# Longer DRAM rows for weight sums and second gate, a margin behind each load's landing in the planner, and 512-column warm-up products, in an attention and two-layer MoE kernel

## The chip, the cores and the metric

One core of one Trainium2 chip. The metric is the device time of one execution in microseconds; the time of a kernel is the median of its runs.

## What is computed

Random-feature attention, whose output is the input of two dense layers in a row. Sizes: 4 batches, 8 heads, 576 tokens, head width 64, 128 features; 2304 tokens of width 512, and an inner width of 2048. All data are fp32. Cut to what matters:

```python
def phi(x):
    proj = np.einsum('bhsd,md->bhsm', x, omega)
    sq = np.sum(x * x, axis=-1, keepdims=True) / 2.0
    h = proj - sq
    h = h - np.max(h, axis=-1, keepdims=True)
    return np.exp(h) / np.sqrt(m)
q_p, k_p = phi(q * scale), phi(k * scale)
kv = np.einsum('bhsm,bhsd->bhmd', k_p, v)
z = np.sum(k_p, axis=2)
num = np.einsum('bhsm,bhmd->bhsd', q_p, kv)
den = np.einsum('bhsm,bhm->bhs', q_p, z)[..., None] + 1e-06
x = (num / den)                      # tokens x 512
...
g = softplus(x @ w_in1);  x = g @ w_out1
g = silu(x @ w_in2);      out = g @ w_out2
```

## The kernel before

**Precision.** PE multiplies in a rounded fp32 form, so each factor is split into a high part (a cast on ACT) and a low part (a subtraction on DVE, `diff`, L285), and each product is three PE products, high·high, high·low and low·high.

**Stages.** Attention comes first. For a batch's keys, pp_k (L579) projects on the features, DVE reduces maxima (L596) and sums of squares (L554), ACT takes the exponential, and pkv (L291) gathers phi·v. For its queries, pp_q, a flip by PE (pq, L745), num (pn, L291), a normalization on DVE (xn, L771) and a transposition back (px, L779) give x in the layout that layer 1 needs. `first_layer` (L849 to 851, tile h) is a plain product of x with w_in1; ACT copies h out of PSUM (L855) and a store puts it to DRAM as `gate[0]`. Attention of batch b+1 is interleaved with layer 1 of batch b.

The other three products use Winograd's scheme: 7 products of 2×2 blocks instead of 8, with combined factors. `second_product(0)` (PE L977) multiplies the softplus of gate 0 with w_out1 and leaves its result in `y_dram`; `first_product` (L1225) multiplies that with w_in2, copies s1, s5, s2 out of PSUM on ACT (L1235), takes the silu and stores `gate[1]`; `second_product(1)` (L983) multiplies gate 1 with w_out2 and writes the output. Each runs the products in the order 1, 5, 6, 2, 7, 3, 4, into the PSUM tiles X, Z and Y. Second products run in NQ = 2 halves of the inner width, each over SC = 3 strips of tokens; a half loads 7 tiles w from `ws` and for each strip 4 tiles b from `gate` (768 KB each, KQ = 4 rows of a pair per partition).

**Sums of weights.** For the three Winograd products `sums_of` makes the 7 combined factors once: it unpacks the raw 64-bit words of two weight chunks to fp32 (DVE and ACT), forms sums (DVE), casts the high part (ACT L456, or L454 with a sign), subtracts the low part (DVE L285), and stores the parts to `ws[m]` in DRAM, m = (0,1), (1,0), (1,1). There are 24 such pairs. In the first APART = 12 of them a store holds 4 or 3 of the 7 factors, in the others 1 or 2. Names: st_11_0_4 is factor 4 of pair 0 of m = (1,1).

**The order of the work.** All instructions of SP, ACT, DVE and PE are added to a list with a cost, a due time and the buffers that they take; class `Order` plays the list against its costs, picks at each step the item with the least due time among those that can start, and the instructions are emitted in the order that comes out. Each engine then runs its own instructions strictly in that order. SP issues nearly all DMAs. In the plan, one wire carries them one after the other, `nbytes / RATE` each, and a DMA ends `ARRIVE` behind its wire time:

```python
if it["nbytes"]:
    wire = max(wire, free[e]) + it["nbytes"] / RATE
    it["end"] = wire + ARRIVE
```

Buffers come in rings by tag (`BUFS`): 2 of "rw", 4 of "ph", 5 of "b2", 4 PSUM banks each of "bank" and "y", and so on; an instruction that opens a tile waits for the last user of the one that held its place. Constants at the top steer the order: `STAY` (PE's inclination to stay with one kind of product), `SLACK`, `FROM`, `EARLY` (how many input tiles take the ring "wa"), `TRAIL`, `EVERY`, `WINDOW_OF`, `FETCH` (when inputs and weights may be fetched), `BACKLOG`, `SOON`, `EARLIER` (loads), `AHEAD`, `WAIT` (projections), `SHARE`, `BEGIN` (due times of layer 1), `PREP` (due times of the sums of weights).

**Warm-up.** Before the first projection, WARM = 2 products of zeros (wz, pw, L325) run on PE while the first loads are under way.

## Time and profile before

| | |
|---|---|
| median of 3 runs | 868.63 us (866.46 to 871.35) |
| profiled execution, its own time | 866.67 us |
| its span | 864.9 us, granted clock 1.0 |
| PE busy | 851.5 us, 98% |
| DVE, ACT busy | 681.6 us (79%), 542.5 us (63%) |
| DMA | 254.54 MB, mean 294 GB/s |

How to read it: one execution, times in us from the start of the span. PE is the matmul engine and PEld its weight loads, which overlap it; DVE, ACT and POOL are the vector, scalar and general engines; SP issues DMAs. In names, a<-b is output from input, xN a count of instructions, L a line of the kernel before. In the changed kernel, the lines from 100 to 465 are numbered 3 higher, and those behind them 4 higher.

### The profile page before, as it was taken

What the parts mean: (1) busy time and instruction counts of PE and PEld (TensorE: products, weight loads), DVE (VectorE), ACT (ScalarE), POOL (GpSimd) and SP (SyncE); (2) the same over time, 40 slices, a digit from 0 to 9 for tenths busy, and PEclk for the clock granted to TensorE, in tenths of its full rate; (3) what the DMA queues carried; (4) which work ended last, traced back from release to release, by engine and by line L of the source; (5) the groups of instructions that cost most, each with busy time, mean ns of one, the idle gap of its engine ahead of it and who ended that gap; (6) DMA issues with size and microseconds to landing.
All of it is one profiled execution on the core that took longest, in us unless ns stands there. A gap on an engine that the chain in (4) does not pass through costs nothing.

```text
span 864.9 us, 17428 instructions
## 1 busy us (share of the span) xinstructions
PE 851.5 (98%) x6492; PEld 801.8 (93%) x6492; DVE 681.6 (79%) x1264; ACT 542.5 (63%) x1088; POOL 1.2 (0%) x8
## 2 busy tenths in 40 slices
PE   8899999999999999999999999999999999999998
PEld 7688888888888899999999998999999999999998
DVE  4999989969997377999799943786754899768973
ACT  6977778768765566876575444766855646543430
POOL 0000000000000000000000000000000000000000
PEclk9999999999999999999999999999999999999999
DMA  9576899899989999979995899987699997799532
GB/s 319 203 240 181 259 314 333 305 348 331 311 297 362 344 345 397 366 258 308 358 324 195 279 354 390 328 291 258 224 317 345 383 352 247 252 348 348 167 117 74
DMA packets 150293, 254.54 MB, mean 294 GB/s; under 512 B 10816, under 2 KB 82624, under 8 KB 150208
## 3 DMA queue, kind: packets, MB, share of 16 engines
q1 hardware_dynamic: 150048, 253.36, 85.0%
q8 instruction: 51, 0.84, 0.4%
q14 instruction: 34, 0.28, 0.1%
q10 hardware_dynamic: 160, 0.07, 0.0%
HBM read 152.72 MB, written 100.66 MB: 293 GB/s over the span
## 4 chain that ended last, share of the span: by engine, by line
PE 89%; DMA 5%; DVE 4%; ACT 1%; issue 1%; SPq 0%; ACTq 0%; DVEq 0%
PE X L977 12%; PE X L983 12%; PE X L1225 8%; PE h L849 8%; PE h L851 8%; PE h L850 8%; PE Z L983 6%; PE Z L977 6%; PE Z L1225 4%; PE Y L983 3%; PE Y L977 3%; PE Y L1225 2%; PE pp_q L579 2%; PE pp_k L579 2%; PE pkv_k L291 2%; PE pn_q L291 2%
## 5 line engine op out<-in xcount | busy, mean ns | idle before, releaser
L849 PE MATMUL h<-x,wt 128*128 128x512 f32 (+1 forms) x328 | 123.4, 376 | 0.0
L851 PE MATMUL h<-x,wt 128*128 128x512 f32 (+1 forms) x328 | 119.6, 365 | 0.0
L850 PE MATMUL h<-x,wt 128*128 128x512 f32 (+1 forms) x328 | 119.4, 364 | 0.0
L1225 PE MATMUL X<-x_x,w 128*128 128x384 f32 x576 | 106.6, 335 | 2.7 <-ACT s L1235 2.4
L925 ACT CAST g<-b 128x768 fp32r<-128x768 f32 x96 | 78.3, 838 | 48.4 <-PE X L983 19.2
L983 PE MATMUL X<-w,g 128*128 128x256 f32 x864 | 107.0, 283 | 0.2 <-issue 0.2
L983 PEld LDWEIGHTS X<-w,g 128*128 128x128 f32 x864 | 105.1, 192 | 0.5 <-issue 0.3
L1225 PEld LDWEIGHTS X<-x_x,w 128*128 128x128 f32 x576 | 100.2, 188 | 3.7 <-ACT s L1235 3.1
L977 PE MATMUL X<-g,w 128*128 128x384 f32 x576 | 102.9, 334 | 0.0
L977 PEld LDWEIGHTS X<-g,w 128*128 128x128 f32 x576 | 100.1, 188 | 0.0
L925 ACT CAST g<-t 128x768 fp32r<-128x768 f32 x72 | 58.8, 834 | 65.3 <-DVE t L910 38.1
L285 DVE TENSOR_TENSOR g<-b,g 128x768 fp32r<-128x768 f32 x96 | 90.0, 951 | 11.1 <-ACT g L925 11.1
L285 DVE TENSOR_TENSOR g<-t,g 128x768 fp32r<-128x768 f32 x72 | 67.5, 953 | 21.0 <-ACT g L925 20.7
L849 PEld LDWEIGHTS h<-x,wt 128*128 128x128 f32 x328 | 61.9, 189 | 10.4
L851 PEld LDWEIGHTS h<-x,wt 128*128 128x128 f32 x328 | 61.9, 189 | 10.2
L285 DVE TENSOR_TENSOR st<-pair,st 128x512 fp32r<-128x512 f32 x72 | 48.9, 686 | 27.9 <-ACT st L456 27.8
L850 PEld LDWEIGHTS h<-x,wt 128*128 128x128 f32 x328 | 62.0, 189 | 8.6
L855 ACT COPY g<-h 128x512 f32<-128x512 f32 (+1 forms) x80 | 44.1, 559 | 28.7 <-PE h L851 20.2
L456 ACT CAST st<-pair 128x512 fp32r<-128x512 f32 x72 | 44.8, 629 | 19.3 <-DMA ws<-st 7.7
L983 PE MATMUL Z<-w,g 128*128 128x256 f32 x432 | 54.0, 283 | 0.2 <-DVE g L285 0.2
L1225 PE MATMUL Z<-x_x,w 128*128 128x384 f32 x288 | 53.8, 334 | 0.0
L983 PEld LDWEIGHTS Z<-w,g 128*128 128x128 f32 x432 | 52.8, 192 | 0.4 <-DVE g L285 0.4
(113 smaller groups left out, 1457.0 us busy)
## 6 DMA issues: line engine op xcount, KB each, us to landing
w<-ws SPq DMA_DIRECT2D x42, 1024.0 KB, 7.7
b<-gate SPq DMA_DIRECT2D x48, 768.0 KB, 7.5
raw<-in_w SPq DMA_DIRECT2D x64, 512.0 KB, 6.0
ws<-st SPq DMA_DIRECT2D x36, 512.0 KB, 5.1
gate<-s SPq DMA_DIRECT2D x96, 192.0 KB, 4.6
gate<-g SPq DMA_DIRECT2D x64, 256.0 KB, 5.0
ws<-st SPq DMA_DIRECT2D x12, 1024.0 KB, 7.0
ws<-st SPq DMA_DIRECT2D x12, 768.0 KB, 5.5
```

What stands on the lines that cost most here:

```text
L285: nc.vector.tensor_tensor(o, a, b, op=ALU.subtract)
L291: nc.tensor.matmul(o[r], a[:, r], b, **flags)
L456: nc.scalar.copy(st[:, :, 0], of())
L579: nc.tensor.matmul(pp[j][:, q], s["xt"][r, c : c + P], om_sb[r, :], start=True, stop=not fold)
L849: nc.tensor.matmul(ph, wt[:, 0, cs], xt[:, 0, ts], start=(opens and cc == 0), stop=False, skip_group_check=part is not None)
L850: nc.tensor.matmul(ph, wt[:, 0, cs], xt[:, 1, ts], start=False, stop=False, skip_group_check=part is not None)
L851: nc.tensor.matmul(ph, wt[:, 1, cs], xt[:, 0, ts], start=False, stop=(cc == NCC - 1), skip_group_check=part is not None)
L855: nc.scalar.copy(s["g"][:, :w], s["h"][:, :w])
L925: nc.scalar.copy(g[:, :, 0], s[src][:, 2 * r : 2 * r + 2])
L977: nc.tensor.matmul(o[:, :HW_], w[:, 2 * r + k, a, cs], g[:, k, h], start=one, stop=(k == 1 and a == 1), skip_group_check=True)
L983: nc.tensor.matmul(o[:, a * 256 : a * 256 + 256], g[:, k, h, ts], w[:, 2 * r + k, v], start=one, stop=(k == 1 and h == 1), skip_group_chec ...
L1225: nc.tensor.matmul(s[x][:, :HW_], w[:, a, cs], xop[p][:, cc, h], start=(opens and cc == 0 and a == 0 and h == 0), stop=(cc == 1 and a == 1 ...
```

## The change

Five things:

1. `gate[1]` is laid out so that a tile b (half, i, strip, j) is one block of DRAM: a load reads rows of 6144 bytes per partition instead of four rows of 1536; the stores still write rows of 1536.
2. `ws[1,0]` is `[128, 56, 512]`: a store's 1 to 4 factors are one row of up to 8 KB per partition, and the load of 4 factors reads 8 KB per partition; the rows of neighbouring partitions lie 56 × 2 KB = 112 KB apart. The other two `ws` are `[NQ, 7, 128, KQ, 512]`: a load reads one block with rows of 8 KB, stores still write rows of 2 KB.
3. The planner's cost of a DMA takes in the length of its rows, and every DMA that starts behind 54.95 us in the plan ends `MARGIN` = 1.11 us later there.
4. Most of the planner's constants have other values.
5. The warm-up products have 512 columns instead of 384.

```diff
-STAY = 6.79
+STAY = 7.6
...
-FROM = {"PE": 4.6, "ACT": 3.4, "DVE": 2.0, "SP": 0.8}
-SLACK = 0.15
-EARLY = 6
+FROM = {"PE": 5.2, "ACT": 3.6, "DVE": 2.0, "SP": 0.8}
+SLACK = 0.09
+EARLY = 3
...
-LEAD, TRAIL, EVERY, WINDOW_OF, FETCH = 0.05, 2.2, 3.13, 25.82, 24.95
+LEAD, TRAIL, EVERY, WINDOW_OF, FETCH = 0.05, 2.42, 3.06, 18.2, 16.35
...
-BACKLOG, SOON = 0.6, 13.16
-EARLIER = (26.31, 42.98)
-APART = 12
-AHEAD, WAIT = 3.04, 4.21
+BACKLOG, SOON = 0.79, 12.44
+EARLIER = (12.06, 21.87)
+APART = 13
+AHEAD, WAIT = 3.8, 4.03
 RATE = 360e3
+PER_BYTE, PER_ROW = 2.44e-6, 6.35e-4
 ARRIVE = 2.3
+MARGIN, FIRM = 1.11, 54.95
...
+        nbytes *= RATE * (PER_BYTE + PER_ROW / row)
...
-                it["end"] = wire + ARRIVE
+                it["end"] = wire + ARRIVE + (MARGIN if s > FIRM else 0.0)
...
-    gate = [dram.tile([NQ, KQ, 2, P, B * S], F32, name=f"gate{i}") for i in range(2)]
+    gate = [dram.tile([NQ, KQ, 2, P, B * S], F32, name="gate0"), dram.tile([NQ, 2, SC, 2, P, KQ, HW_], F32, name="gate1")]
...
-    ws = {m: dram.tile([NFP, 7, P, 2 * 256], F32, name=f"ws{m[0]}{m[1]}") for m in ((0, 1), (1, 0), (1, 1))}
+    ws = {m: dram.tile([P, NFP * 7, 2 * 256] if m == (1, 0) else [NQ, 7, P, KQ, 2 * 256], F32, name=f"ws{m[0]}{m[1]}") for m in ((0, 1), (1, 0), (1, 1))}
...
-    wz = get("b2", [P, 3 * P], F32, "wz")
+    wz = get("b2", [P, 2 * T], F32, "wz")
...
-                nc.sync.dma_start(ws[m][k, g : g + rows].rearrange("o p w -> p o w"), q["st"].bitcast(F32).rearrange("p o h w -> p o (h w)"))
+                to = ws[m][:, 7 * k + g : 7 * k + g + rows] if m == (1, 0) else ws[m][k // KQ, g : g + rows, :, k % KQ].rearrange("o p w -> p o w")
+                nc.sync.dma_start(to, q["st"].bitcast(F32).rearrange("p o h w -> p o (h w)"))
...
-                    nc.sync.dma_start(s["b", i, j], gate[layer][q, :, i, :, lo:hi].rearrange("k p t -> p k t"))
+                    nc.sync.dma_start(s["b", i, j], gate[1][q, i, sc, j] if layer else gate[0][q, :, i, :, lo:hi].rearrange("k p t -> p k t"))
...
-                nc.sync.dma_start(w.bitcast(F32).rearrange("p k h w -> p k (h w)"), ws[1, 0].rearrange("k o p w -> (k o) p w")[o : o + 4].rearrange("k p w -> p k w"))
+                nc.sync.dma_start(w.bitcast(F32).rearrange("p k h w -> p k (h w)"), ws[1, 0][:, o : o + 4])
...
-                        nc.sync.dma_start(gate[1][fc // (2 * KQ), fc // 2 % KQ, fc % 2][:, lo : lo + HW_], s[key])
+                        nc.sync.dma_start(gate[1][fc // (2 * KQ), fc % 2, sc, j, :, fc // 2 % KQ], s[key])
```

Since the planner's numbers change, all four engines' orders change. Three places:

On DVE, at the start (mn the maxima of a projection pp, sqs the sums of squares, kv0 the copy of pkv), before:

```order
L596 TENSOR_REDUCE mn_k0_0_0_165<-pp_k0_0_0_122 128x4
L596 TENSOR_REDUCE mn_k0_0_1_168<-pp_k0_0_1_123 128x4
L596 TENSOR_REDUCE mn_k1_0_0_185<-pp_k1_0_0_145 128x4
L596 TENSOR_REDUCE mn_k1_0_1_197<-pp_k1_0_1_146 128x4
L596 TENSOR_REDUCE mn_k0_1_0_237<-pp_k0_1_0_199 128x4
L663 COPY kv0_98<-pkv_k0_0_187 128x260
L596 TENSOR_REDUCE mn_k0_1_1_268<-pp_k0_1_1_200 128x4
L554 TENSOR_REDUCE sqs_q0_0_278<-x_q0_0_107 128x8
L554 TENSOR_REDUCE sqs_kt0_286<-x_kt0_106 128x8
L596 TENSOR_REDUCE mn_k1_1_0_296<-pp_k1_1_0_250 128x4
```

and after the change:

```order
L600 TENSOR_REDUCE mn_k0_0_0_165<-pp_k0_0_0_122 128x4
L600 TENSOR_REDUCE mn_k0_0_1_168<-pp_k0_0_1_123 128x4
L600 TENSOR_REDUCE mn_k1_0_0_202<-pp_k1_0_0_145 128x4
L600 TENSOR_REDUCE mn_k1_0_1_206<-pp_k1_0_1_146 128x4
L600 TENSOR_REDUCE mn_k0_1_0_228<-pp_k0_1_0_177 128x4
L600 TENSOR_REDUCE mn_k0_1_1_248<-pp_k0_1_1_178 128x4
L600 TENSOR_REDUCE mn_k1_1_0_264<-pp_k1_1_0_230 128x4
L667 COPY kv0_98<-pkv_k0_0_214 128x260
L600 TENSOR_REDUCE mn_k1_1_1_292<-pp_k1_1_1_231 128x4
L558 TENSOR_REDUCE sqs_q0_0_294<-x_q0_0_107 128x8
```

The reduces of pp_k0_1 and pp_k1_1 stand ahead of the copy to kv0, and the reduce sqs_kt0 no longer stands among them (it and sqs_k3_0 come later, sqs_k3_0 behind the last xn of the first batch).

On PE, in the attention of the second batch between gemms of layer 1 (pp_q2_0 and pp_q2_1 are projections of queries, pkv_k3_1 a product of keys and values), before:

```order
L579 MATMUL pp_q2_0_1_1097<-om_sb_86,x_q2_0_761 128x128
L579 MATMUL pp_q2_0_0_1096<-om_sb_86,x_q2_0_761 128x128
L579 MATMUL pp_q2_0_1_1097<-om_sb_86,x_q2_0_761 128x128
L291 MATMUL pkv_k3_1_1113<-x_k3_1_670,phi_k3_1_0_1031 64x65 x8
L291 MATMUL pkv_k3_1_1113<-x_k3_1_670,phi_k3_1_1_1038 64x65 x8
L579 MATMUL pp_q2_1_0_1134<-om_sb_86,x_q2_1_886 128x128
L579 MATMUL pp_q2_1_1_1135<-om_sb_86,x_q2_1_886 128x128
L579 MATMUL pp_q2_1_0_1134<-om_sb_86,x_q2_1_886 128x128
```

and after:

```order
L583 MATMUL pp_q2_0_1_1062<-om_sb_86,x_q2_0_814 128x128
L583 MATMUL pp_q2_0_0_1061<-om_sb_86,x_q2_0_814 128x128
L583 MATMUL pp_q2_0_1_1062<-om_sb_86,x_q2_0_814 128x128
L583 MATMUL pp_q2_1_0_1080<-om_sb_86,x_q2_1_944 128x128
L583 MATMUL pp_q2_1_1_1081<-om_sb_86,x_q2_1_944 128x128
L583 MATMUL pp_q2_1_0_1080<-om_sb_86,x_q2_1_944 128x128
L583 MATMUL pp_q2_1_1_1081<-om_sb_86,x_q2_1_944 128x128
L583 MATMUL pp_q2_1_0_1080<-om_sb_86,x_q2_1_944 128x128
```

The two projections now stand one behind the other, and pkv_k3_1 comes later, behind the gemms h_0_4 and h_0_5. Over the whole kernel the runs of pp products fall from 33 to 29, those of pkv and pn from 36 to 34, and those of the gemm rise from 41 to 43.

On ACT, at the start of the first product of layer 2 (s1, s5, s2 copies out of PSUM and their silus, st_11_0_* the casts of the first pair of weight sums for the last product), before:

```order
L1235 COPY s2_0_2_6405<-X_0_2_6341 128x384
L1235 COPY s2_0_3_6414<-X_0_3_6356 128x384
L1245 ACTIVATE s1_0_2_6364<-s1_0_2_6364 128x384
L1245 ACTIVATE s1_0_3_6377<-s1_0_3_6377 128x384
L1245 ACTIVATE s5_0_2_6389<-s5_0_2_6389 128x384
L456 CAST st_11_0_4_6453<-pair_11_0_6130 128x2x256
L1245 ACTIVATE s5_0_3_6397<-s5_0_3_6397 128x384
L456 CAST st_11_0_2_6463<-pair_11_0_6130 128x2x256
L1245 ACTIVATE s2_0_2_6405<-s2_0_2_6405 128x384
L1245 ACTIVATE s2_0_3_6414<-s2_0_3_6414 128x384
L1251 ACTIVATE s4_0_2_6487<-X_0_2_6341 128x384
L1251 ACTIVATE s4_0_3_6498<-X_0_3_6356 128x384
```

and after:

```order
L1176 CAST x3_x2_0_6108<-r110_x2_0_5686 128x384
L1176 CAST x3_x2_0_6108<-r111_x2_0_5696 128x384
L1176 CAST x4_x2_0_6122<-tb_x2_0_5861 128x384 x2
L459 CAST st_11_0_0_6191<-pair_11_0_6058 128x2x256
L457 ACTIVATE st_11_0_6_6200<-pair_11_0_6058 128x256
L1239 COPY s1_0_0_6234<-X_0_0_6214 128x384
L1239 COPY s1_0_1_6244<-X_0_1_6226 128x384
L1239 COPY s5_0_0_6253<-Z_0_0_6237 128x384
L1239 COPY s5_0_1_6261<-Z_0_1_6246 128x384
L1239 COPY s2_0_0_6269<-X_0_0_6214 128x384
L1239 COPY s2_0_1_6278<-X_0_1_6226 128x384
L459 CAST st_11_0_4_6290<-pair_11_0_6058 128x2x256
```

The four casts st_11_0_* of that pair stood among the silus of the first and second pair of units (two of them are in the rows of before); now two stand ahead of the first copies s1, and the other two among the first pair's.

## Rows read from the trace of the kernel before

**Rows 1.** Page, busy time by engine and the chain's shares.

```profile
PE 851.5 (98%) x6492; PEld 801.8 (93%) x6492; DVE 681.6 (79%) x1264; ACT 542.5 (63%) x1088; POOL 1.2 (0%) x8
...
PE 89%; DMA 5%; DVE 4%; ACT 1%; issue 1%; SPq 0%; ACTq 0%; DVEq 0%
```

**Rows 2.** Busy time by stretch: length, each engine (instructions), PEclk, DMA share, GB/s.

```profile
0.00:20.00 20.00, 17.72 (x230) 15.26 (x230) 7.92 (x14) 13.49 (x41) 1.20 (x8) 1.00 0.94 313
20.00:46.00 26.00, 21.26 (x337) 18.04 (x336) 24.97 (x84) 24.41 (x72) 0.00 (x0) 1.00 0.63 222
46.00:120.00 74.00, 74.00 (x712) 62.25 (x710) 70.28 (x171) 56.71 (x138) 0.00 (x0) 1.00 0.73 232
120.00:300.00 180.00, 180.00 (x1494) 150.02 (x1491) 147.90 (x376) 128.34 (x309) 0.00 (x0) 1.00 0.94 331
520.00:560.00 40.00, 38.08 (x220) 37.76 (x219) 20.99 (x43) 23.46 (x51) 0.00 (x0) 1.00 1.00 362
560.00:640.00 80.00, 80.00 (x463) 80.00 (x463) 57.25 (x116) 55.56 (x119) 0.00 (x0) 1.00 0.78 267
640.00:680.00 40.00, 39.26 (x228) 38.52 (x227) 22.48 (x43) 23.33 (x49) 0.00 (x0) 1.00 1.00 349
680.00:720.00 40.00, 39.76 (x330) 39.40 (x329) 38.06 (x47) 23.97 (x41) 0.00 (x0) 1.00 1.01 364
760.00:800.00 40.00, 39.83 (x333) 39.66 (x332) 31.51 (x38) 15.19 (x20) 0.00 (x0) 1.00 1.00 344
800.00:865.00 65.00, 61.59 (x514) 61.39 (x512) 44.77 (x59) 19.09 (x24) 0.00 (x0) 0.99 0.39 119
```

**Rows 3.** PE's waits: total us, times, longest.

```profile
PE px_q L779 <- DVE xn_q L771: 3.8, 3, 1.8
```

**Rows 4.** Timeline of PE at the start: start, us, what, idle before.

```profile
1.81 2.93 PE L325 MATMUL pw<-wz,ident 128*128 128x384 f32 x4 [1.81 <-POOL ident masks.py:199]
5.21 0.80 PE L579 MATMUL pp_k<-om_sb,x_k 64*128 64x128 f32 x4 [0.47 <-ACT om_sb L320]
```

**Rows 5.** Chain of waits, 10 to 11 us: start, us, what.

```profile
10.37 0.43 PE pp_k L583 x4
...
11.08 0.22 PE pp_k L583 x4
```

**Rows 6.** Busy time, 9 to 19.2 us, columns as in rows 2.

```profile
9.00:19.20 10.20, 10.20 (x184) 9.63 (x184) 7.12 (x13) 8.86 (x31) 0.00 (x0) 1.00 1.08 369
```

**Rows 7.** Chain of waits, one reduce on DVE at 43.7 us.

```profile
43.70 0.60 DVE sqs_k L554
```

**Rows 8.** Chain of waits, short and long runs of one kind on PE.

```profile
11.75 0.61 PE pkv_k L291 x16
...
14.35 1.08 PE pkv_k L291 x32
...
181.44 1.99 PE pp_k L579 x32
...
192.90 1.09 PE pp_k L579 x16
```

**Rows 9.** Chain of waits, 519 to 540 and 667 us.

```profile
519.91 8.74 DMA ws<-st
...
530.80 8.68 DMA gate<-s
...
539.56 0.49 ACT s L1235
...
667.43 7.34 DMA b<-gate
```

**Rows 10.** Timeline of ACT, the cast at 528.7 us.

```profile
528.73 0.62 ACT L456 CAST st<-pair 128x512 fp32r<-128x512 f32 x1 [2.87 <-DMA ws<-st]
```

**Rows 11.** Page, DMA issues: count, KB each, median us to landing.

```profile
w<-ws SPq DMA_DIRECT2D x42, 1024.0 KB, 7.7
b<-gate SPq DMA_DIRECT2D x48, 768.0 KB, 7.5
```

More of the change, by code (lines that the diff above doesn't have):

```diff
@@ L95, in __init__, with add @@
         self.items = []
-    def add(self, eng, cost, fn, deps=(), due=None, alloc=(), uses=(), table=None, nbytes=0, after=0.0, loose=False, behind=None, wait=0.0, tiled=False, turn=None):
+    def add(self, eng, cost, fn, deps=(), due=None, alloc=(), uses=(), table=None, nbytes=0, after=0.0, loose=False, behind=None, wait=0.0, tiled=False, turn=None, row=2048):
         occ, lag = cost if isinstance(cost, tuple) else (cost, PIPE)
         i = len(self.items)
+        nbytes *= RATE * (PER_BYTE + PER_ROW / row)
         it = dict(
@@ L380, in unpack @@
         opens = not tf["users"]
-        a = add("SP", (ISSUE, 0), load, alloc=[traw], nbytes=P * DM * 8, after=after, due=due)
+        a = add("SP", (ISSUE, 0), load, alloc=[traw], nbytes=P * DM * 8, row=4096, after=after, due=due)
         b = add("ACT", (0.575, 0.37), scale, [a], alloc=[tf] if opens else [], uses=[traw] + ([] if opens else [tf]))
@@ L474, in stage @@
             if not q["left"]:
-                kept[m, k].append(add("SP", (ISSUE, 0), store, q["ends"], uses=[ts], nbytes=P * 256 * rows * 8, due=due))
+                kept[m, k].append(add("SP", (ISSUE, 0), store, q["ends"], uses=[ts], nbytes=P * 256 * rows * 8, row=2048 * (rows if m == (1, 0) else 1), due=due))
             return b
@@ L543, in load_v @@
                 nc.sync.dma_start(s["v", i], v)
-            lv.append(add("SP", (ISSUE, 0), load_v, rv if tw is here else [] if opens else lv[:1], alloc=[tv[i]] if opens else [], uses=[] if opens else [tv[i]], nbytes=P * VW * 4, after=after))
+            lv.append(add("SP", (ISSUE, 0), load_v, rv if tw is here else [] if opens else lv[:1], alloc=[tv[i]] if opens else [], uses=[] if opens else [tv[i]], nbytes=P * VW * 4, row=1040 if shape[1] == 4 else 2080, after=after))
         def square():
@@ L898, in load @@
                     s["b", i, j] = get("xg", [P, KQ, HW_], F32, f"b{i}{j}_{name}")
-                    nc.sync.dma_start(s["b", i, j], gate[layer][q, :, i, :, lo:hi].rearrange("k p t -> p k t"))
-                got[i, j] = add("SP", (ISSUE, 0), load, deps, alloc=[tb[i, j]], nbytes=P * n * 4)
+                    nc.sync.dma_start(s["b", i, j], gate[1][q, i, sc, j] if layer else gate[0][q, :, i, :, lo:hi].rearrange("k p t -> p k t"))
+                got[i, j] = add("SP", (ISSUE, 0), load, deps, alloc=[tb[i, j]], nbytes=P * n * 4, row=HW_ * 4 * (KQ if layer else 1))
                 if layer == 0:
@@ L1009, in load @@
                     nc.sync.dma_start(s["h", c, i, j][:, : wide[c]], part_of(c, i, j))
-                return add("SP", (ISSUE, 0), load, [partly[sc, c, i, j]], alloc=[ht], nbytes=P * wide[c] * 4)
+                return add("SP", (ISSUE, 0), load, [partly[sc, c, i, j]], alloc=[ht], nbytes=P * wide[c] * 4, row=wide[c] * 4)
             def snap(p, x, c, i, j, due):
@@ L1055, in store @@
                                 nc.sync.dma_start(out[r0 : r0 + n, cs], s["h", c, i, j][p0 : p0 + n, a * 256 : a * 256 + 256])
-                            add("SP", (ISSUE, 0), store, [e], uses=[ht], due=due + 3, nbytes=n * 1024)
+                            add("SP", (ISSUE, 0), store, [e], uses=[ht], due=due + 3, nbytes=n * 1024, row=1024)
                 return e
@@ L1103, in load_w @@
                     w = wt[p] = get(tag, [P, KQ, 2, 256], F32R, f"w2_{layer}_{q}_{p}")
-                    nc.sync.dma_start(w.bitcast(F32).rearrange("p k h w -> p k (h w)"), ws[wm][q * KQ : (q + 1) * KQ, ROW[p]].rearrange("k p w -> p k w"))
-                wload[p] = add("SP", (ISSUE, 0), load_w, [i for k in range(q * KQ, (q + 1) * KQ) for i in kept[wm, k]], alloc=[tws[p]], nbytes=P * KQ * 2048, turn=t0, after=t0 + n * each - EARLIER[layer])
+                    nc.sync.dma_start(w.bitcast(F32).rearrange("p k h w -> p k (h w)"), ws[wm][q, ROW[p]])
+                wload[p] = add("SP", (ISSUE, 0), load_w, [i for k in range(q * KQ, (q + 1) * KQ) for i in kept[wm, k]], alloc=[tws[p]], nbytes=P * KQ * 2048, row=8192, turn=t0, after=t0 + n * each - EARLIER[layer])
             for sc in range(SC):
```

20 lines of the change are left out of this document (10 added, 10 removed).

## The prediction

> **What bounds the kernel now.** I read four views, in this order. The first is the page's busy table with the shares of the chain of waits [rows 1]: PE is busy 851.5 of 864.9 us, 89% of the chain is PE's work, and DVE and ACT are far from full over the whole. So the kernel is bound by PE, and only two things can shorten it: less PE work, or less of the 864.9 − 851.5 = 13.4 us in which PE stands still. The second view, busy time by stretch, says where these lie [rows 2]: length minus PE's busy time gives 2.28 us up to 20, 4.74 from 20 to 46, nothing from 46 to 300 (two stretches full to the last digit; from 300 to 520 no stretch is shown, since it reads the same), 1.92 from 520 to 560, 0.74, 0.24 and 0.17 in the stretches at 640, 680 and 760, and 3.41 behind 800. The third, PE's waits [rows 3] and the busy time from 20 to 46 [rows 2], says what bounds the start: there DVE is busy 24.97 of 26 us, and PE's largest wait is on DVE's xn_q (3.8 us). The fourth, the chain with ACT's timeline, explains the late stall, below.
>
> Durations come from the profiled execution, whose own time is 866.67 us; the median shown is 868.63, 1.96 above it. About 0.5% (4.3 us) is what a measurement of this kernel can tell from no change.
>
> **The change part by part.** PE executes the same products before and after; what changes is their order, the warm-up, and where data lie in DRAM.
>
> (a) *DVE's start.* From 20 to 46 us DVE sets PE's pace, so a DVE instruction that is moved from ahead of the first products of layer 1 to behind them shortens this part by its duration. The order shows one: the reduce of squares sqs_k3_0 now stands behind the last xn that the first gemm needs. One takes 0.60 us [rows 7]. −0.6.
>
> (b) *PE's start.* The projections pp_k0_1 stand ahead of pkv_k0_0 now, so that DVE's reduces on them no longer wait for a product that only the copy to kv needs: a short run of pkv is 0.61 us [rows 8]. The gain reaches the end only if DVE then works earlier, and DVE's idle time from 9 to 19.2 us, 10.20 − 7.12 = 3.08 us [rows 6], is all that (b) and (c) together can take. Between 0 and −0.6 I take −0.6, since DVE waits in just this stretch.
>
> (c) *Warm-up.* Four matmul records of pw take 2.93 us at 384 columns, PE then stands 0.47 us for om_sb, and the first projections start at 5.21 [rows 4]. 512 columns cost a third more, 0.98 us, of which 0.47 fill the gap: +0.5. Against this stands PE's speed: a block of four projection matmuls takes 0.43 us up to 10.8 us and 0.22 from 11.08 [rows 5], a factor of 1.95, though the granted clock stands at 1.00 for the whole stretch [rows 2]. I read the first as the level of 1.2 GHz and the second as 2.4. The slow blocks fill 5.21 to 10.80 = 5.59 us; if the rise came with the longer warm-up at once, half of that, 2.8 us, would be saved. The ends are +0.5 (no earlier rise) and 0.5 − 2.8 = −2.3; I take −0.5, a rise some 2 us sooner, near the cautious end, because no row shows what brings the rise on.
>
> So the start gives −0.6 − 0.6 − 0.5 = −1.7.
>
> (d) *Fewer changes of kind on PE.* A run of 16 pp matmuls takes 1.09 us and one of 32 takes 1.99, so 16 more cost 0.90 and a run has 0.19 fixed; for pkv it is 0.61 and 1.08, 0.14 fixed [rows 8]. By the order, runs of pp fall from 33 to 29 and runs of pkv and pn from 36 to 34; the gemm runs between them rise from 41 to 43, which I count with these pairs and not again. They lie where PE is full from 46 to 300 [rows 2], so each counts whole: −4 × 0.19 − 2 × 0.14 = −1.0. Beside this, moved gemms could make PE wait for DVE, which is busy 70.28 of 74 us from 46 to 120 [rows 2]; I cost this at nothing, as 3.7 us of idle time cover it, and at up to +1.5 in the range if they do not.
>
> (e) *The late waits.* At 528.73 ACT's cast into st_11_0_4 has waited 2.87 us for a store ws<-st to leave its buffer [rows 10]; that store was issued at 519.91 and took 8.74 us to land. ACT then takes up what is queued behind the cast, the copies s of the first product of layer 2, whose buffers in turn wait for the store gate<-s (530.80, 8.68 us); the copy that PE needs ends near 540 [rows 9]. That is PE's 1.92 us. From 520 to 560 the DMA engines are busy all the time at 362 GB/s [rows 2], so stores land late because loads stand ahead of them, not because ACT is full (23.46 of 40). The change moves the four casts of this pair ahead of the copies and their stores some 20 us earlier, and the planner counts 1.11 us more for each landing. I take the 1.92 as gone. What is late next are the small stalls, 0.74 + 0.24 + 0.17 = 1.15 us, which hang on the same kind of landing: 667.43, a b<-gate took 7.34 us [rows 9]. The margin is made for them, but each order trades one for another; I take a quarter, −0.3. Ends: nothing gained, and −3.1. Together −2.2.
>
> (f) *Longer rows.* The 42 loads of 1 MB and the 48 of 768 KB land in a median of 7.7 and 7.5 us [rows 11], in rows of 2048 and 1536 bytes. Nearly all lies under PE's work, so a shorter transfer shows only through the waits in (e) and is not counted again: 0. If loads got slower, the cover is the free share of the stretches between full ones: 560 to 640 has a DMA share of 0.78 [rows 2], so 17.6 us of wire. The output stores behind the last product (most of the 3.41 us) are not touched.
>
> Sum: −1.7 − 1.0 − 2.2 = −4.9, that is 866.67 − 4.9 = 861.8 on the profiled execution, and 868.63 − 4.9 = 863.7 on the median. The profiled execution lies at the low end of the runs, so I take a value between the two, **863.0 us**, 0.65% faster than the median shown.
>
> **The rivals.**
>
> *The waits only move (chance 0.25).* The start is DVE's work, which is nearly unchanged (24.97 of 26), and a planner that packs DMAs differently makes another late store. For it: the late stalls all follow from queues full at 349 to 364 GB/s [rows 2], and neither bytes nor rate need change. Then only (a) and (d) stay, −1.6: 866.67 − 1.6 = 865.1 to 868.63 − 1.6 = 867.0; I put it at 866.5, since a late wait can also grow.
>
> *Slower: the long pitch of ws[1,0] (chance 0.07).* Its tensor is now [128 partitions, 56 rows of 2 KB], so neighbouring partitions lie 112 KB apart, where a row of 2 KB once followed the next. No row of before shows such a pitch. 14 loads of 1 MB read it from the third stage on. At 362 GB/s [rows 2] one is 2.9 us of wire; at half the rate the 14 need 14 × 2.9 = 40.6 us more, against 17.6 free us between 560 and 640: about 23 us fall on PE, 868.63 + 23 = 891.6 or 889.7 on the profiled base, less the 4.9: about 885. It decides once a load's wire time exceeds 2.9 + 17.6 / 14 = 4.2 us. Against it: a partition now reads its 8 KB in one piece, where today's rows of 2 KB let 1 MB land in 7.7 us [rows 11]. The Trainium skill, "DMA: Bandwidth & Descriptors", section "Latency and other measured facts", tells of such a loss for row pitches at large powers of two: copies at a pitch of 512 KiB ran at 207 GB/s, at 4 MiB at 103. 112 KiB is no power of two and smaller than all of these, so by its wording this pitch would not fall under the rule; no run here shows it yet.
>
> *More comes off (chance 0.13).* The clock level rises as soon as the projections begin (−2.3 in place of −0.5) and all late waits go (−3.1 in place of −2.2): −4.9 − 1.8 − 0.9 = −7.6, so 859.1 to 861.0; 859.5. The Trainium skill, "TensorE: Matmul & The Clock Gate", section "What's actually happening", says that the throttled state is the default and that activity releases it, which would favour a longer warm-up. In this trace PE's warm-up ran from 1.81 to 4.74 and the fast blocks came only near 11 [rows 4, 5], so the rule alone does not say that another microsecond brings it forward; by it (c) would be −2.3.
>
> **How the numbers follow.** The forecast has 0.55, the rivals 0.25, 0.07 and 0.13. The forecast's own weak end has (b) at nothing, (c) at +0.5 and of (e) the 1.9 alone, −0.6 + 0.5 − 1.0 − 1.9 = −3.0, 865.6 on the median; its strong end is the third rival. The range from 858.5 (more comes off) to 869.0 (the waits only move, or DVE is late by 1.5 after 46) leaves out the slow case and the tails, 0.2 in all. Faster by over 0.5% means below 864.3: most of the forecast (0.40 of 0.55), all of the third rival (0.13) and a little of the first (0.01), 0.54. Slower by over 0.5% means above 873.0: 0.07 and 0.01 of mishap, 0.08. The rest, 0.38, is no change that can be told.
>
> **What would show it.** In the profile after: PE's idle time up to 46 us about 5.3 instead of 7.0 with the same products done; 0.43 us blocks that end before 9 us (c); PE's busy sum from 46 to 300 less by 1.0 (d); no ACT cast that waits for ws<-st near 528 and no idle PE from 520 to 560 (e); w<-ws landing no later than now (f). The prediction is wrong if late stretches keep over 2 us of idle PE, if the first gemm starts no earlier, or if w<-ws for layer 2 lands in over 10 us.

## The result, and the profile after

The changed kernel takes **859.96 us** (median of 6 runs, 859.32 to 861.46) against 868.48 us of the kernel before (6 runs, 866.46 to 871.35): a ratio of 0.9902, 95% interval 0.988 to 0.9924, so 1.0% faster. The forecast was 863.0 us with a range of 858.5 to 869.0: the direction and the range were right, the gain was larger than forecast (8.5 us, or 6.4 between the two profiled executions, 866.67 and 860.29, against the 4.9 of its sum). Beside the median the spread changed: 4.9 us before, 2.1 us after.

The page of the changed kernel, busy time by engine and the chain's shares, answers to [rows 1]:

```profile
PE 848.8 (99%) x6492; PEld 799.6 (93%) x6492; DVE 683.8 (80%) x1264; ACT 544.8 (63%) x1088; POOL 1.3 (0%) x8
...
PE 94%; DVE 3%; DMA 2%; ACT 0%; issue 0%; POOL 0%; POOLq 0%; DVEq 0%; ACTq 0%
```

PE executes as many instructions as before; its share of the chain rose from 89% to 94%, and DMA's fell from 5% to 2%. The busy time by stretch, with the columns of [rows 2], says where:

```profile
0.00:20.00 20.00, 18.08 (x280) 14.86 (x282) 9.07 (x19) 14.52 (x45) 1.31 (x8) 1.00 0.95 327
20.00:46.00 26.00, 21.45 (x304) 18.06 (x299) 24.87 (x81) 23.68 (x69) 0.00 (x0) 1.00 0.64 216
46.00:120.00 74.00, 74.00 (x685) 61.61 (x685) 69.38 (x171) 57.37 (x144) 0.00 (x0) 1.00 0.72 236
120.00:300.00 180.00, 180.00 (x1519) 150.58 (x1514) 145.88 (x372) 126.71 (x304) 0.00 (x0) 1.00 0.92 324
520.00:560.00 40.00, 40.00 (x232) 40.00 (x231) 27.07 (x53) 27.05 (x58) 0.00 (x0) 1.00 1.00 369
560.00:640.00 80.00, 80.00 (x463) 80.00 (x463) 53.13 (x106) 52.84 (x112) 0.00 (x0) 1.00 0.67 230
640.00:680.00 40.00, 39.92 (x248) 39.72 (x247) 26.87 (x43) 24.81 (x50) 0.00 (x0) 1.00 1.01 377
680.00:720.00 40.00, 40.00 (x334) 39.85 (x333) 37.40 (x47) 26.06 (x42) 0.00 (x0) 1.00 0.93 358
760.00:800.00 40.00, 40.00 (x336) 40.00 (x335) 33.70 (x41) 16.24 (x21) 0.00 (x0) 1.00 0.94 342
800.00:859.00 59.00, 55.31 (x461) 55.11 (x460) 38.92 (x53) 15.85 (x20) 0.00 (x0) 0.98 0.33 98
```

The late idle time of PE, 1.92 + 0.74 + 0.24 + 0.17 us before [rows 2], is 0.08 us. DMA is no less busy: from 520 to 560 and 640 to 680 its engines are still full. The start has 1.92 + 4.55 = 6.47 us of idle PE instead of 7.02, where the prediction named 5.3 as its sign: PE executes the same 562 matmuls ahead of the first gemm, and of the 1.53 us that this gemm comes earlier, 0.55 are idle time and the rest busy time, though the warm-up is 0.85 us longer.

In stages, by the start of each stage's first product in the two traces (before, after, difference):

| stage | before | after | difference |
|---|---|---|---|
| start to first gemm of layer 1 | 45.88 | 44.35 | −1.53 |
| first gemm to second product of layer 1 | 279.96 | 279.40 | −0.56 |
| second product of layer 1 | 174.73 | 174.72 | 0 |
| first product of layer 2 | 178.35 | 174.72 | −3.63 |
| second product of layer 2, to PE's last | 182.67 | 182.12 | −0.55 |

The same two places on ACT that stood behind the stall of 1.92 us [rows 9, 10], in the timeline of ACT of the changed kernel:

```profile
507.02 0.62 ACT L459 CAST st<-pair 128x512 fp32r<-128x512 f32 x1 [1.63 <-DMA ws<-st]
...
514.84 0.96 ACT L1239 COPY s<-X 128x384 f32<-128x384 f32 x2 [1.04 <-DMA gate<-s]
```

Both waits are still there, 1.63 us on a store ws<-st where it was 2.87, and 1.04 on gate<-s, where three copies of the kernel before waited 5.60 us in all; from the timeline of ACT of the kernel before:

```profile
534.59 0.86 ACT L1235 COPY s<-Z 128x384 f32<-128x384 f32 x2 [1.96 <-DMA gate<-s]
537.64 0.48 ACT L1235 COPY s<-X 128x384 f32<-128x384 f32 x1 [2.20 <-DMA gate<-s]
539.56 0.48 ACT L1235 COPY s<-X 128x384 f32<-128x384 f32 x1 [1.44 <-DMA gate<-s]
```

The waits come earlier and are shorter, and what is queued behind them on ACT reaches PE in time.

The page's DMA lines answer to [rows 11]:

```profile
w<-ws SPq DMA_DIRECT2D x42, 1024.0 KB, 8.0
b<-gate SPq DMA_DIRECT2D x48, 768.0 KB, 7.3
```

Longer rows left the landings where they were (7.7 and 7.5 before); the 0.3 us more of w<-ws are within what the old rows show from kernel to kernel, 7.7 to 8.4 on their pages. PE's start, from the timeline of PE, beside [rows 4, 5]:

```profile
1.92 3.78 PE L328 MATMUL pw<-wz,ident 128*128 128x512 f32 x4 [1.92 <-POOL ident masks.py:199]
5.63 0.80 PE L583 MATMUL pp_k<-om_sb,x_k 64*128 64x128 f32 x4
...
7.40 0.39 PE L583 MATMUL pp_k<-om_sb,x_k 64*128 64x128 f32 x4
7.62 0.39 PE L587 MATMUL pp_k<-neg_half,x_k 64*128 64x128 f32 x4
```

The warm-up runs into the projections without a gap, and blocks of four start every 0.22 us from 7.40 on, where it was from about 10.8 on before. PE's wait on DVE's xn_q at the start fell from 3.8 us [rows 3] to 2.9.

### The profile page after: what moved, and what is told of

Read it like the earlier page. It is cut to its first block, busy times and chain, and to the rows that moved or that the text cites. A ratio compares the mean times of both kernels' runs of the same rounds, so it can differ in the third digit from the quotient of the medians.

```text
span 858.5 us, 17419 instructions
## 1 busy us (share of the span) xinstructions
PE 848.8 (99%) x6492; PEld 799.6 (93%) x6492; DVE 683.8 (80%) x1264; ACT 544.8 (63%) x1088; POOL 1.3 (0%) x8
## 2 busy tenths in 40 slices
DMA packets 120565, 254.54 MB, mean 296 GB/s; under 512 B 10784, under 2 KB 70304, under 8 KB 114464
## 4 chain that ended last, share of the span: by engine, by line
PE 94%; DVE 3%; DMA 2%; ACT 0%; issue 0%; POOL 0%; POOLq 0%; DVEq 0%; ACTq 0%
PE X L981 12%; PE X L987 12%; PE X L1229 10%; PE h L853 8%; PE h L855 8%; PE h L854 8%; PE Z L987 6%; PE Z L981 6%; PE Z L1229 5%; PE Y L987 3%; PE Y L981 3%; PE Y L1229 3%; PE pp_q L583 2%; PE pp_k L583 2%; PE pn_q L294 2%; DMA ws<-st 2%
## 5 line engine op out<-in xcount | busy, mean ns | idle before, releaser
L1249 ACT ACTIVATE s<-s 128x384 f32<-128x384 f32 x72 | 37.5, 525 | 29.4 <-DVE s L1244 29.2
```

The lines of the kernel that those rows point to most:

```text
L1249: a = add("ACT", on_act(HW_), lambda: nc.scalar.activation(s[key], s[key], AF.Silu), [dep], uses=[th], due=due, table="silu")
```

## The experiments

My theory was that the late waits are a matter of the order, and the rest small terms at the start. The rivals were that longer rows shorten the landings, that one pair of weight sums was the whole late matter, and that the warm-up did more or less than its term. Twelve experiments were run in three groups, each group on a chip of its own. The kernel before, timed in each, had medians of 870.17 us (29 runs, 864.15 to 874.02), 870.66 (18) and 870.45 (11), some 2 us above the runs shown ahead; ratios are against the runs of the same group. The first group's expectations count from 868.5 us, so they are read here as distances from 870.17.

**The longer rows alone.** The kernel before with the layouts of `gate[1]` and `ws`, their stores and their loads as in the change, and the old planner:

```diff
-    gate = [dram.tile([NQ, KQ, 2, P, B * S], F32, name=f"gate{i}") for i in range(2)]
+    gate = [dram.tile([NQ, KQ, 2, P, B * S], F32, name="gate0"), dram.tile([NQ, 2, SC, 2, P, KQ, HW_], F32, name="gate1")]
-    ws = {m: dram.tile([NFP, 7, P, 2 * 256], F32, name=f"ws{m[0]}{m[1]}") for m in ((0, 1), (1, 0), (1, 1))}
+    ws = {m: dram.tile([P, NFP * 7, 2 * 256] if m == (1, 0) else [NQ, 7, P, KQ, 2 * 256], F32, name=f"ws{m[0]}{m[1]}") for m in ((0, 1), (1, 0), (1, 1))}
...
```

> The kernel before with the new DRAM layouts of the weight sums and of gate 1 alone; its order of instructions, planner and warm-up stay as they were. If the late waits are a matter of the order (my theory), it stays within 1 us of the kernel before (868.5 us), and PE's idle time from 520 to 560 us stays between 1.2 and 2.2 us. If longer rows shorten the landings (first rival), ws<-st and gate<-s near 520 to 531 land in under 7 us instead of 8.7, the idle time there falls below 0.5 us, and the time falls by 2 to 4 us, to 864.5 to 866.5. If the 112 KB pitch of ws[1,0] costs anything, loads w<-ws from 500 us on land over 2 us later than before and the time is above 869.5.

Measured: 870.4 us (12 runs, 865.97 to 872.79), ratio 0.9995 (0.9972 to 1.0017): the rows alone do nothing that can be told. The order of instructions on PE, ACT, DVE and SP is that of the kernel before (its L1236 is L1235 of before), and yet in its profiled execution the stalls stand at other places. The chain of waits at one of them:

```profile
523.92 9.46 DMA ws<-st
...
535.47 6.73 DMA gate<-s
542.28 0.49 ACT s L1236
```

It is the same story as [rows 9, 10] with a store that took 9.46 us in place of 8.74, so the landings did not shorten. From 500 to 680 us PE stood still for 5.7 us, against 2.7 in the kernel before; from 520 to 560 it was 1.09, a little below the 1.2 expected. The 14 loads that read `ws[1,0]` at its pitch of 112 KB landed in a median of 8.3 us here and 7.1 in the kernel before, but with the old layout they took 8.0 and 9.1 in the traces of the warm-up alone and of the one due time, below, and 9.0 in the new order, where the new layout has 8.5. So the pitch costs nothing that shows.

**The order without the rows.** The changed kernel with the old layouts; the same edit turned round.

> The changed kernel with the old DRAM layouts; its order of instructions and its warm-up stay those of the changed kernel. By my theory (order) it takes 859 to 861.5 us, within 1 us of the changed kernel (860.0), with no PE idle time above 0.2 us at any place between 46 and 680 us. By the first rival (rows) late waits come back: 862 to 864 us, with 1 to 3 us of PE idle time between 500 and 800 us.

Measured: 860.11 us (5 runs, 859.66 to 861.35), ratio 0.9886 (0.9865 to 0.9907). PE's only late wait in its trace (columns: us in total, times, longest; lines here are numbered 1 lower than in the changed kernel):

```profile
PE Z L986 <- DVE g L288: 0.7, 1, 0.7
```

It stands at 677 us, where the expectation allowed 0.2 at most up to 680; the changed kernel waits 0.08 us at that place. So nearly the whole gain comes with the order and the warm-up, and the layouts' part is below the resolution of some 2 us in both directions. Put in alone and left out alone, the rows say the same, which is why they are settled to that limit.

**One due time.** The kernel before, with the casts and stores of the first pair for the last product earlier, as the change has them:

```diff
-PREP = (118.5, 128.9, 155.1, 144.2, 172.5, 186.4, 193.1, 218.5, 239.1, 242.1, 258.9, 272.1, 289.7, 296.7, 311.4, 322.8, 520.9, 537.5, 578.5, 584.0, 604.5, 622.5, 614.1, 638.6)
+PREP = (118.5, 128.9, 155.1, 144.2, 172.5, 186.4, 193.1, 218.5, 239.1, 242.1, 258.9, 272.1, 289.7, 296.7, 311.4, 322.8, 512.7, 537.5, 578.5, 584.0, 604.5, 622.5, 614.1, 638.6)
```

> The kernel before with one number of the planner changed: the due time of the first pair of weight sums for the last product is 512.7 us instead of 520.9, as in the change, so that its four casts and stores stand earlier on ACT and SP. By my theory the 1.92 us of PE idle time from 520 to 560 go and the smaller stalls near 657, 677, 683 and 779 us (together 1.6 to 2 us) stay: 866 to 867 us. If the stall has another cause (loads in the queue, not these casts), it stays or moves, and the time is within 0.7 us of 868.5.

Measured: 870.1 us (12 runs, 866.53 to 874.18), ratio 0.9992 (0.9976 to 1.0009). My theory of this stall expected 866 to 867: a miss. From 520 to 560 PE's idle time did fall from 1.92 to 0.36 us, but PE's waits in the profiled execution say what took its place:

```profile
PE Z L983 <- DVE g L285: 2.8, 1, 2.8
PE X L1225 <- DVE s L1240: 2.0, 1, 2.0
```

The second stands at 515 us, where the chain of waits runs over a store ws<-st of this pair, issued at 503.67, that took 10.28 us; the first at 686 us, where PE waits for a factor g of DVE. DVE had worked without a break since 678.63, where it had lost 2.15 us to ACT, and ACT to a load b<-gate that took 7.34 us; from the timeline of DVE:

```profile
678.63 0.96 DVE L285 TENSOR_TENSOR g<-b,g 128x768 fp32r<-128x768 f32 x1 [2.15 <-ACT g L925]
```

Moving one pair moves the wait. This profiled execution, 874.18 us, is the slowest of its 12 runs.

**The warm-up alone.** The kernel before with products of 512 columns:

```diff
-    wz = get("b2", [P, 3 * P], F32, "wz")
+    wz = get("b2", [P, 2 * T], F32, "wz")
-    pw = get("bank", [P, 3 * P], F32, "pw")
+    pw = get("bank", [P, 2 * T], F32, "pw")
```

> The kernel before with warm-up products of 512 columns instead of 384 and nothing else. If the longer warm-up brings TensorE's fast level forward, as it came near 7 us in the changed kernel and near 11 in the kernel before, the slow blocks of projections end before 8 us here too, and the first gemm of layer 1 starts 0 to 1.0 us earlier than at 45.88 (the rest of the 1.53 us being the order's). If the earlier rise came from the changed order on PE, slow blocks last until near 11 us and the first gemm starts 0 to 0.5 us later. The median moves by less than 1 us either way, and all stalls behind 500 us stay.

Measured: 869.9 us (12 runs, 865.44 to 872.17), ratio 0.9987 (0.9967 to 1.0008). Blocks of 0.22 us come from 6.3 us on, as expected (before 8), and DVE's first maximum starts at 7.84 us instead of 9.12. At 44.7 us DVE is still 0.9 us ahead of the one-due-time kernel, which has the old warm-up; yet the first gemm starts at 46.02 us, 0.49 later than there and 0.14 later than in the kernel before, where up to 1.0 earlier was expected. The busy time from 36 to 48 us of this execution has the reason in its PEclk column (the column behind POOL):

```profile
36.00:42.00 6.00, 3.42 (x30) 2.44 (x31) 5.79 (x18) 5.94 (x17) 0.00 (x0) 0.74 0.05 11
42.00:48.00 6.00, 6.00 (x68) 5.71 (x68) 5.60 (x17) 2.44 (x6) 0.00 (x0) 0.69 0.93 311
```

The granted clock was 0.74 and 0.69 there, a mean between full speed (2.4 GHz) and the level of 1.2 GHz: part of the time PE ran at the lower one. PE had stood still for 1.66 us for xn_q just before; but it had for 1.74 us at the same place in the one-due-time kernel, where the clock stayed at 1.00. The projections that stand ahead of the last px took 2.02 us, against 1.16 in the one-due-time kernel at full clock; timeline of PE of each:

```profile
43.87 2.02 PE L579 MATMUL pp_k<-om_sb,x_k 64*128 64x128 f32 x16
```

```profile
43.70 1.16 PE L579 MATMUL pp_k<-om_sb,x_k 64*128 64x128 f32 x16
```

So the longer warm-up alone gains nothing that can be told in the old order: it brings the first 40 us forward by about 0.9 us, and the clock takes that back before the first gemm. Each of these is one execution, and that of the warm-up alone, 872.17 us, is the slowest of its 12 runs. The clock fell in the same way in one other trace, below.

**The margin alone.** The kernel before with one term in the planner:

```diff
-                it["end"] = wire + ARRIVE
+                it["end"] = wire + ARRIVE + (1.11 if s > 54.95 else 0.0)
```

> The kernel before with the planner's margin alone: every DMA that starts behind 54.95 us in the plan ends 1.11 us later there; all other numbers, the layouts and the warm-up as before. Theory M (the margin is what keeps late landings from PE): the time falls to 861.5 to 864.5 us and its runs lie within 3 us of each other, where those of the kernel before spread over 864 to 874; PE stands still less than 1 us in all between 500 and 800 us. Rival C (the other late constants, due times of the weight sums and the earliest times of loads, do it): 868 to 870.5 us, a spread of over 5 us, and 3 us or more of PE idle time between 500 and 800.

Measured: 866.32 us (7 runs, 865.75 to 867.95), ratio 0.9944 (0.9921 to 0.9967). The spread fell from 11 us (864.81 to 875.84 for the kernel before in this group) to 2.2, as theory M says; the time fell by about half of what it said, and PE stood still for 1.5 us between 500 and 800, where under 1 was expected. Its trace has no idle PE in the first product of layer 2, which takes 174.72 us as in the changed kernel, but two waits elsewhere:

```profile
PE X L983 <- DVE g L285: 1.5, 1, 1.5
PE X L977 <- DVE g L285: 0.9, 1, 0.9
```

By stages, PE's last product ends 6.40 us later in its profiled execution than in that of the changed kernel in the third group: 2.70 of these lie ahead of the first gemm, 1.05 between this and the second product of layer 1, and 2.65 in the two second products, where the two waits above stand.

**The change without the margin.**

```diff
-MARGIN, FIRM = 1.11, 54.95
+MARGIN, FIRM = 0.0, 54.95
```

> The changed kernel with the margin set to 0; all other numbers, the layouts and the warm-up as in the changed kernel. Theory M: late waits come back, 863 to 868 us with a spread of over 4 us and 2 us or more of PE idle time between 500 and 800 us. Rival C: 859.5 to 861.5 us with a spread below 2.5 us and less than 1 us of PE idle time there.

Measured: 867.04 us (12 runs, 864.56 to 873.47), ratio 0.9969 (0.9946 to 0.9991). Late waits and the spread are back, 4.0 us of idle PE between 500 and 800. PE's longest waits:

```profile
PE X L987 <- DVE g L288: 1.8, 1, 1.8
PE Z L987 <- DVE g L288: 1.1, 1, 1.1
```

So the margin is worth some 7 us within the change, and 4.3 us (870.66 − 866.32) alone; everything but the margin is worth 3.6 us (870.66 − 867.04). Together they give 10.8 (870.45 − 859.68, from the next group), 2.8 more than the two apart. It may be that the other constants pay fully only where the margin keeps the late landings away, but each of the three gains is known to about 2 us only, so this is not shown.

**The late constants without the early ones.** The changed kernel with the old values of the constants for attention and layer 1:

```diff
-STAY = 7.6
+STAY = 6.79
-FROM = {"PE": 5.2, "ACT": 3.6, "DVE": 2.0, "SP": 0.8}
-SLACK = 0.09
-EARLY = 3
+FROM = {"PE": 4.6, "ACT": 3.4, "DVE": 2.0, "SP": 0.8}
+SLACK = 0.15
+EARLY = 6
...
-LEAD, TRAIL, EVERY, WINDOW_OF, FETCH = 0.05, 2.42, 3.06, 18.2, 16.35
+LEAD, TRAIL, EVERY, WINDOW_OF, FETCH = 0.05, 2.2, 3.13, 25.82, 24.95
...
-AHEAD, WAIT = 3.8, 4.03
+AHEAD, WAIT = 3.04, 4.21
...
-BEGIN = 34.87
-SHARE = (1.77, 1.19, 0.93, 0.39, 0.32)
+BEGIN = 38.66
+SHARE = (1.76, 1.19, 1.06, 0.07, 0.19)
```

> The changed kernel with the old values of those constants that set the order of attention and layer 1 (STAY, FROM, SLACK, EARLY, TRAIL, EVERY, WINDOW_OF, FETCH, AHEAD, WAIT, BEGIN, SHARE); margin, row costs, load constants, due times of the weight sums, layouts and warm-up stay as in the changed kernel. If the early part of my sum (start and fewer changes of kind) was right, 1 to 2.5 us of the gain go: 861 to 862.5, with the first gemm at 45 to 46 us and the stretch from it to the second product 0.4 to 0.9 us longer. If the whole gain is in the late waits, it stays within 0.7 us of 860. If the early constants also keep later waits away, it is above 864.

Measured: 863.12 us (4 runs, 861.94 to 864.87), ratio 0.9911 (0.9887 to 0.9935), between two of its branches (861 to 862.5, and above 864). The first gemm starts at 46.09 us, 1.74 later than in the changed kernel, and layer 1 takes 280.65 us against 279.40, 1.25 longer: somewhat more than the 0.4 to 0.9 expected. The late start has the same reason as with the warm-up alone; the busy time from 36 to 48 us:

```profile
36.00:42.00 6.00, 3.59 (x34) 2.59 (x30) 5.79 (x18) 5.94 (x18) 0.00 (x0) 0.74 0.05 8
42.00:48.00 6.00, 6.00 (x67) 5.65 (x67) 5.70 (x18) 2.56 (x5) 0.00 (x0) 0.69 0.89 298
```

Both traces with the old early constants and the long warm-up have this fall of the clock, and none of the other ten experiments has it, nor the kernel before, nor the changed one. The rest is a late wait of 1.7 us at the second product of layer 2; the chain of waits ahead of it:

```profile
668.37 10.81 DMA b<-gate
```

Since the early constants shift what follows, the plan behind is another one. A long landing by itself is no stall: in the changed kernel two gate loads issued at 682 and 683 us took 12.78 and 13.93 us, and PE waited 0.08 us in all between 500 and 800. That the order decides whether a late load is waited for is what this suggests; it was not tested apart.

**The changed kernel again, and two other margins.** The constant is 1.11, then 0.55, then 1.8:

```diff
-MARGIN, FIRM = 1.11, 54.95
+MARGIN, FIRM = 0.55, 54.95
```

> The changed kernel once more, as the base of this group on the same chip: 859 to 862 us, runs within 2.5 us of each other, under 0.3 us of PE idle time between 46 and 670 us.

> The changed kernel with half the margin, 0.55 us instead of 1.11. If the margin works as a distance that late landings use up, the time lies between that of no margin (867.0 us) and that of the changed kernel (860): 861.5 to 865.5 us, with a spread of 2.5 to 6 us. If 1.11 is only a lucky number, one order among many, it may come out anywhere from 859 to 868, the spread with it.

> The changed kernel with a margin of 1.8 us instead of 1.11. If the margin works as a distance, no late wait is left to be saved, so the time stays within 1 us of the changed kernel (859.5 to 861.5), unless the plan puts its own waits in to keep the larger distance: then 861 to 864, with PE idle time that is the same in every run (a spread below 2.5 us). If 1.11 is only a lucky number: over 863 us with a spread above 4 us.

Measured, with the margin of 0 from the group before (the changed kernel came as expected):

| margin, us | median, us | lowest to highest | runs | ratio to the kernel before |
|---|---|---|---|---|
| 0 | 867.04 | 864.56 to 873.47 | 12 | 0.9969 (0.9946 to 0.9991) |
| 0.55 | 861.13 | 858.76 to 863.15 | 6 | 0.9893 (0.9875 to 0.9911) |
| 1.11 | 859.68 | 859.22 to 860.36 | 4 | 0.9878 (0.986 to 0.9896) |
| 1.8 | 863.43 | 862.13 to 864.22 | 6 | 0.9918 (0.9901 to 0.9935) |

The half margin is nearer to the whole one than expected (861.5 to 865.5), with a single run below all of the changed kernel's. The larger one loses 3.8 us again, as one branch of its expectation said: a narrow spread around a longer time. Its longest late wait by PE's waits:

```profile
PE Z L987 <- DVE g L288: 1.8, 1, 1.8
```

So up to 1.11 the runs fit a margin that works as a distance which late landings use up; beyond that the plan, which believes its own later landings, pays elsewhere. Each margin is one order of instructions, so a share of luck in a single value is not excluded; against mere luck stands that the spread fell with the margin in the old order too. That 1.8 us wait, at 677.9 us, where the changed kernel waits 0.08, is in one profiled execution; that it recurs in each run is only argued from the spread of 2.1 us.

**The short warm-up in the new order.** The changed kernel with 384 columns, first in the second group without the changed kernel beside it, then again in the third with it:

> The changed kernel with the old warm-up of 384 columns and nothing else. By my prediction's term the time rises by about 0.5 us, to 860.5, with slow projections until near 11 us and the first gemm at 44.5 to 45.5 us. If the warm-up's gain is lost on the way (as it was when put into the kernel before), it stays within 0.3 us of 860.0; if PE's start sets the first gemm fully, the time rises by 1.3 us or more.

> The changed kernel with the warm-up of 384 columns again, now beside the changed kernel on the same chip, since its 861.46 us had none beside it. If the longer warm-up is worth my term of 0.5 us, it is 0.2 to 0.9 us slower than the changed kernel of this group; if the earlier time was the chip's, within 0.2 us; if the warm-up is worth more, 1 to 2 us slower.

Measured: 861.46 us (4 runs, 860.84 to 862.42, ratio 0.9891, 0.9869 to 0.9913) and 861.77 us (5 runs, 859.38 to 862.6, ratio 0.9899, 0.9881 to 0.9917). Beside the changed kernel's 859.68 this is 2.1 us slower by the medians, above even the largest branch of the last expectation, but the intervals of the ratios overlap and one run, at 859.38, is as fast as the changed kernel. Over all groups, eight of nine runs with 384 columns lie at 860.84 us or above, and nine of ten of the changed kernel at 860.36 or below. So the longer warm-up gains in the new order; 1 to 2 us is an estimate from these runs. The two profiled executions of this kernel differ from each other: the first gemm starts at 44.32 us in one and at 46.32 in the other. The timeline of PE of the second, where the 0.22 us steps come late:

```profile
6.44 0.80 PE L583 MATMUL pp_k<-om_sb,x_k 64*128 64x128 f32 x4 [1.70 <-ACT om_sb L323]
...
10.11 0.55 PE L583 MATMUL pp_k<-om_sb,x_k 64*128 64x128 f32 x4
10.50 0.39 PE L587 MATMUL pp_k<-neg_half,x_k 64*128 64x128 f32 x4
```

and that of the first of the two, where they come soon after 6.6 us (slow blocks until near 11 were expected), though the gap behind the warm-up is nearly as long:

```profile
6.07 0.49 PE L583 MATMUL pp_k<-om_sb,x_k 64*128 64x128 f32 x4 [1.32 <-ACT om_sb L323]
6.59 0.49 PE L587 MATMUL pp_k<-neg_half,x_k 64*128 64x128 f32 x4
6.91 0.39 PE L583 MATMUL pp_k<-om_sb,x_k 64*128 64x128 f32 x4
```

The start of the projections hangs on om_sb, whose last load landed 3.46 us after its issue in the kernel before and 4.68 us after it in the second of these two traces; so the speed of PE is read better from the time between the first projection and DVE's first maximum, which is behind the same products in all traces. With 384 columns it is 3.91 us in five of six traces and 2.38 in one, with 512 it is 2.28 to 3.26 in all eight. So the longer warm-up makes the early 0.22 us steps the rule, where with the shorter one they came early once in six. The granted clock reads 1.00 in all of these stretches, with slow steps and with fast ones; that the two steps are the clock's two levels stays a reading from their ratio.

## Why the prediction was right, and where it was off

**(a) to (c), the start, forecast −1.7, measured −1.53 in the two traces.** The start has three parts: up to the first projection, from there to DVE's first maximum, and from this to the first gemm. In the two traces they went from 5.21, 3.91 and 36.76 us to 5.63, 2.86 and 35.86. The first two belong to (c), the warm-up: +0.42 − 1.05 = −0.63 against −0.5. The third holds (a) and (b), the order: −0.90 against −1.2. So both terms were near in these two traces. All fourteen traces, in us:

| early constants, warm-up | traces | first projection | to first maximum | to first gemm |
|---|---|---|---|---|
| old, 384 | 4 | 5.21 to 5.73 | 3.91 | 36.42 to 36.78 |
| old, 512 | 2 | 5.46, 5.63 | 2.38, 3.26 | 38.18, 37.20 |
| new, 384 | 2 | 6.07, 6.44 | 2.38, 3.91 | 35.87, 35.97 |
| new, 512 | 6 | 5.42 to 5.93 | 2.28 to 2.86 | 35.85 to 35.88 |

The order's part is there in every trace with the new early constants, with either warm-up: 0.8 us between the means. The warm-up's part, 1.0 to 1.6 us in the middle column, is kept with the new early constants; with the old ones the granted clock fell from 36 to 48 us and the last column gave 0.4 us or more of it back. That the two first gemms with the new constants and 384 columns stand 2 us apart (44.32 and 46.32) comes from the first two columns, not from the order. How (a) and (b) share the 0.8 was not tested. The 0.22 us steps came near 7 us in the changed kernel, some 3.5 us earlier, nearly the far end of (c), but the gain was not the 2.3 us of that end: the slow blocks up to DVE's first maximum took 3.91 us, so about half of these, and not of 5.59, was what DVE could gain.

The Trainium skill, "TensorE: Matmul & The Clock Gate", section "What's actually happening", says that activity releases the throttle. The traces agree in direction, if the 0.22 us steps are the released level: behind the longer warm-up the first maximum came 2.28 to 3.26 us after the first projection, against 3.91 in five of six traces with the shorter one.

**(d) Fewer changes of kind, forecast −1.0, measured −0.56** from the first gemm to the second product in the two traces; against four of the other old-order traces (280.39 to 280.97) it is −1.0 to −1.6, since these hold 0.1 to 0.7 us of idle PE there. In busy time alone, the old early constants have 280.0 to 280.4 us in six traces and the new ones 278.8 to 279.7 in eight, 0.9 less in the mean, so the size was about right. That fewer changes of kind are the reason is not shown. The term left out the flips pq, whose runs rise from 22 to 24; from the first gemm to the second product the runs of all kinds fall from 141 to 139 only, and the kernels with 136 runs there have both 278.79 and 279.73 us of busy time. The sign named for (d), less busy time from 46 to 300 us, could not show it, since PE is full there before and after.

**(e) The late waits, forecast −2.2, measured −4.2** (−3.63 − 0.55). This is the step that was mis-sized, in two ways. First, PE's idle time undercounts a stall: by the distance between the starts of one matmul and the next, the seven irregular places in the first product of layer 2 lost 3.53 us, where its idle time is 2.66. Second, and larger, I took the waits of one execution for the kernel's. That execution took 866.67 us, close to the fastest of those shown, and I noted it and went to a value between it and the median, without asking why the runs spread over 5 us. The traces say that the late waits differ from run to run: the stretch from the start of the second product of layer 1 to PE's last product took 535.75 us in the trace shown, 538.91 and 540.35 in two others with the same order (the rows alone, the warm-up alone), and 542.6 with one due time moved; in the changed kernel it took 531.56 and 531.55. So the waits to be saved were 4 to 9 us in the old order, and the spread of its runs was the sign of it.

The reason was half right. A store that lands late under a full queue, a cast that waits for it on ACT, and the copies behind it: that is what the traces show in the first product of layer 2 in all four executions of the old order without the margin. But I put it down to the pair st_11_0, and moving this pair alone (one due time) only moved the wait, to 515 and 686 us. What ends it is the margin all through the plan: with it alone the spread falls from 11 to 2.2 us, and the change without it has 8.9. In the prediction's sum the margin stood beside the moved casts for the 1.92 us, and by itself for a quarter of the small stalls, 0.3; it measured 4.3 us alone and some 7 within the change.

**(f) Longer rows, forecast 0: right.** A ratio of 0.9995 alone, and 860.11 us without them. The sign named for it, w<-ws landing no later, failed by 0.3 us (8.0 after 7.7), but the new order with the old rows has 8.3, and the second trace of the changed kernel 7.7, so the rows are not the reason.

**The rivals.** That the waits only move (0.25) holds for one pair alone, and not for the change. The slow case from the pitch (0.07) did not come: its 14 loads landed in a median of 8.3 and 8.5 us with it, and 7.1 to 9.1 without. The Trainium skill's row on pitches at large powers of two ("DMA: Bandwidth & Descriptors", "Latency and other measured facts") is not contradicted: 112 KB is none. The case that more comes off (0.13, 859.5) has nearly the measured time, but in part by luck. All late waits went, as its second half says, and they were worth 4.2 us where it had 3.1; of its first half, a start of −0.6 − 0.6 − 2.3 = −3.5, the two traces have −1.53.

## What to carry to other kernels

Where the runs of a kernel spread by more than a wait that you see in its trace, the trace holds one draw of several: price the waits from the spread of the runs, not from one execution. The median minus the fastest run is a lower bound, since the fastest can hold waits too: 2.0 us in the runs shown ahead, where 8.5 came off. A static order that is planned to the exact landing of a DMA loses to the landings that come later than planned; here a margin on each landing bought both median and spread, and one that was too large cost part of it again. Before you move the one instruction that stands ahead of a stall, ask what the next late landing will hit.
